# A window attention and two MLPs on one core: the first batch's attention in another order, two steps with plain float32 products, and no GpSimd work on the first block or on weights

## The chip, the core and the metric

The kernel runs on one core of one Trainium2 chip. A core has TensorE (PE in the profile, with its weight loads as PEld), VectorE (DVE), ScalarE (ACT), GpSimd (POOL) and SyncE (SP), each with an instruction queue of its own that is worked off in order, and DMA queues. All DMAs of this kernel are issued from SP. The metric is the device time of one execution in microseconds. The kernel before takes 1016.48 us (median of 3 runs, 1015.5 to 1017.78).

## The reference

Four batches of 8 heads with 512 local and 32 global tokens, head size 64. A global token attends to all 544 keys; a local token attends to the 32 global keys and to the local keys at most 32 places away. The heads are put side by side to 2176 rows of 512 (the layers after it are written for 2304 tokens; the kernel's own count is 4 x (512 + 32) = 2176).

```python
attn_out = _attn_ref(**attn_kwargs)               # softmax(q k^T / 8) v, windowed + global
x = attn_out.transpose(0, 2, 1, 3).reshape(B * S, H * D)
# _moe_ref: 512 -> 1536 -> 512
rms = np.sqrt(np.mean(x * x, axis=-1, keepdims=True) + 1e-06)
xn = x / rms * rms_g
g = xn @ w_gate
silu = g * (1.0 / (1.0 + np.exp(-g)))
x = (silu * (xn @ w_val) @ w_out).astype(np.float32)
# _moe2_ref: 512 -> 2048 -> 512
h = x @ w_in
out = (np.maximum(0.01 * h, h) @ w_out).astype(np.float32)
```

The weights of both MLPs reach the chip as float64 and everything else as float32.

## The kernel before, in words

**Weights.** A weight tile of 128 x 512 comes in as pairs of 32-bit words. `narrow` (L93) makes float32 of it in three instructions: `nc` on ScalarE (L104), `nr` on VectorE (L110) or GpSimd (L107), and `wf` on VectorE (L112). Then `split` makes two fp32r halves of it: `high` is a ScalarE cast (L75), `low` a subtraction (L83) on GpSimd for weights. A product of two float32 matrices is `mm3` (L68 to L71): three matmuls high x high, low x high, high x low.

**Blocks.** The 2176 columns (tokens) go through the first MLP in five blocks (512 and four times 416 columns), each in twelve steps f of 128 hidden units: gate `pg` and value `pv` (four mm3 each), then the product of the step before with its output weights, `yp` (four mm3). Block 0 narrows and splits each step's three weight tiles (k = 0, 1, 2 for gate, value, output) and writes the halves to `w1_dram`; blocks 1 to 4 only fetch them. The second MLP then runs over five blocks of at most 512 columns in 16 steps each (`ph`, `tl`, `h2h`/`h2l`, `o`); its own weights (`w64b`, `nr_b`, `wfb`, `w0h`, `w0l`, ...) are narrowed and split during block 4 (the first six steps' worth) and in the first 10 steps that follow.

**Attention.** Batch 0's attention runs ahead of block 0; batch b+1's is spread over block b's steps by the table `PLAN`. A unit is two heads; a half unit k has scores `S` (matmuls, VectorE min/mask L232, ScalarE exp L235), `N` (the softmax's division, L241 to L244), `T` (transposes and the copies `pt0`, `pt1` to SBUF, L257: `pt0` on ScalarE, `pt1` on VectorE) and `V` (`po`, copied into `x_loc`). `G` are the five parts of two units' global queries. The string `ORDER` lists these parts for batch 0. After each unit's `V`, `D` calls `squares` of that 128-row chunk; when the four are there `root` (L451) has TensorE sum them over partitions (`pm`), ScalarE takes the root (L459, after a table load) and VectorE the reciprocal `rv` (L461). Step 0's gate and value use `xg`, x times the gain, as two halves (L419 on GpSimd and L420 on VectorE), and its results are multiplied by `rv`; from step 1 on the operand is x normalised (`xn` L467, `xh` on ScalarE, `xl` on GpSimd).

**Order.** The kernel's text gives each engine's instructions; a scheduler that simulates the engines then decides the final order on each queue, within the dependences, the buffer counts (`bufs`) and the pins (`issue_after`, `pinned`).

Of the kernel before, what the change touches and what calls it, by code (L numbers as in the profile page):

```python
# [16 lines left out]
P = 128  # L17
# [6 lines left out]
def tile_window_global_attention_two_mlps(  # L24
# [48 lines left out]
    def high(eng, hi, src):  # L73
        if eng == "act":
            return nc.scalar.copy(hi, src)  # L75
        elif eng == "pool":
            nc.gpsimd.tensor_scalar(out=hi, in0=src, scalar1=1.0, scalar2=0.0, op0=ALU.mult, op1=ALU.add)
        else:
            nc.vector.tensor_copy(hi, src)

    def low(eng, lo, src, hi):
        e = nc.gpsimd if eng == "pool" else nc.vector
        e.tensor_tensor(out=lo, in0=src, in1=hi.bitcast(F32), op=ALU.subtract)  # L83

    def split(hi, lo, src, e_hi, e_lo):
        high(e_hi, hi, src)
        low(e_lo, lo, src, hi)
# [5 lines left out]
    def narrow(pool, dst, raw, name, e_r="dve"):  # L93

        c = pool.tile([P, DM], F32, tag="nar_c", bufs=2, name="nc_" + name)
        r = pool.tile([P, DM], U32, tag="nar_r", bufs=2, name="nr_" + name)
        nc.scalar.activation(out=c, in_=raw[:, :, 1].bitcast(F32), func=AF.Prelu, scale=2.0 ** -112,  # L104
                             alpha=-2.0 ** 32)
        if e_r == "pool":
            nc.gpsimd.tensor_scalar(out=r, in0=raw[:, :, 0], scalar1=0.93 * 2.0 ** -29, scalar2=0.03,  # L107
                                    op0=ALU.mult, op1=ALU.add)
        else:
            nc.vector.tensor_scalar(out=r, in0=raw[:, :, 0], scalar1=2.0 ** -29, scalar2=7.0,  # L110
                                    op0=ALU.mult, op1=ALU.min)
        nc.vector.scalar_tensor_tensor(out=dst.bitcast(U32), in0=c.bitcast(U32), scalar=3, in1=r,  # L112
                                       op0=ALU.logical_shift_left, op1=ALU.bitwise_or)
# [96 lines left out]
    def half_unit(k):  # L210
# [36 lines left out]
        def turned(j):  # L247
# [9 lines left out]
            (nc.vector.tensor_copy if j else nc.scalar.copy)(pt, pp)  # L257

        def values():
# [9 lines left out]
            (nc.scalar.copy if b < 2 else nc.vector.tensor_copy)(x_loc[b][:, p, c0:c0 + 2 * P], po[:, 0:2 * P])  # L269
# [83 lines left out]
    def attention(b, unit_done=None):  # L353
# [3 lines left out]
        globs = {w: global_pair(k0 // 4 + w) for w in range(NP // 2)}  # L357

        def one(t):
# [5 lines left out]
            if t[0] == "G":  # L365
                return globs[n]["1n234".index(t[2])]
# [10 lines left out]
        if not b:  # L377
            return [item(t) for t in ORDER.split()]
        return {(f, int(q)): [item(t) for t in texts.split()]
                for f, slots in PLAN.items() for q, texts in (x.split(":") for x in slots.split(";"))}  # L380

# [32 lines left out]
    def gained(c, n):  # L414
        src, g = x_loc[0][:, c, 0:n], gcol[:, c:c + 1]
        if c == 0:
            xg.extend(mp.tile([P, KC, NX], F32R, tag=f"x{y}", bufs=2, name=f"xg{y}") for y in "hl")
        hi, lo = (x[:, c, 0:n] for x in xg)
        (nc.vector if c == KC - 1 else nc.gpsimd).tensor_scalar(out=hi, in0=src, scalar1=g, scalar2=None, op0=ALU.mult)  # L419
        later(lambda: nc.vector.scalar_tensor_tensor(out=lo, in0=src, scalar=g, in1=hi.bitcast(F32),  # L420
                                                     op0=ALU.mult, op1=ALU.subtract))

    def normalise(i, c0, n):
# [40 lines left out]
        def scaled(c):  # L464
# [5 lines left out]
            high("act", xs[i][0][:, c, 0:n], xn[:, 0:n])  # L470
            later(lambda: low("pool" if i < 1 else "dve", xs[i][1][:, c, 0:n], xn[:, 0:n], xs[i][0][:, c, 0:n]))
# [14 lines left out]

    def fetch(g, k):
# [13 lines left out]

    def convert(g, k):
# [3 lines left out]
        wf[g, k] = mp.tile([P, DM], F32, tag="wf", bufs=5, name=f"wf{k}_{g}")  # L506
        with pinned({0: f"n{2 * NP - 1}", 1: "sqrt"}.get(f, "")):
            narrow(mp, wf[g, k], wraw[g, k], f"{k}_{f}", "pool" if k and f > 1 else "dve")
        if step_of(g + 1)[0] == 0:
            if g == 0:  # L510
                with tc.issue_after(loads[5, 1].ins):
                    fetch(g + 1, k)
            else:
                fetch(g + 1, k)

    def prep(g, k):

        i, f = step_of(g)
        if i == 0:
            t = weight_tile(g, k)  # L520
            split(t[:, 0, :], t[:, 1, :], wf[g, k], "act", "pool")
            nc.sync.dma_start(out=w1_dram[f][k], in_=t.bitcast(F32))
            convert(g + 1, k)

# [47 lines left out]
    def rows_in(i, c):  # L572
# [16 lines left out]

    def ahead():  # L590
# [4 lines left out]
        for f in range(6):  # L595
            for k in range(2):
                jobs.append(lambda f=f, k=k: weights2(f, k, pre2[0], mp, f"w64{(2 * f + k) % 3}"))
        for c in range(KC):
            jobs.insert(2 * (c + 1) - 1, lambda c=c: rows_in(0, c))
        return jobs  # L600

    def mlp1(early):
# [8 lines left out]
        for g in range(NI * NF1):  # L611
# [107 lines left out]
    c0 = 0  # L719
# [97 lines left out]
```

## Time and profile before

| | |
|---|---|
| time, median of 3 runs | 1016.48 us (1015.5 to 1017.78) |
| profiled execution: its own time, its span | 1016.41 us, 1014.6 us |
| mean granted TensorE clock | 0.977 |
| PE, DVE, ACT, POOL busy | 961.3, 500.5, 391.2, 159.0 us |
| first exp, last exp of batch 0's attention begin (ACT) | 6.36, 52.36 us |
| reciprocal `rv` begins (DVE) | 69.88 us |
| step 2's gate begins (PE) | 104.58 us |
| block 1 begins, second MLP begins (PE) | 219.5, 618.3 us |

The span runs from the first to the last instruction; the execution's own time has 1.8 us more, outside of all instructions. Times in the rows are us from the span's start. The granted clock is given as a share of full speed.

### The profile page before, as it was taken

What the parts mean: (1) busy time and instruction counts of PE and PEld (TensorE: products, weight loads), DVE (VectorE), ACT (ScalarE), POOL (GpSimd) and SP (SyncE); (2) the same over time, 40 slices, a digit from 0 to 9 for tenths busy, and PEclk for the clock granted to TensorE, in tenths of its full rate; (3) what the DMA queues carried; (4) which work ended last, traced back from release to release, by engine and by line L of the source; (5) the groups of instructions that cost most, each with busy time, mean ns of one, the idle gap of its engine ahead of it and who ended that gap; (6) DMA issues with size and microseconds to landing.
All of it is one profiled execution on the core that took longest, in us unless ns stands there. A gap on an engine that the chain in (4) does not pass through costs nothing.

```text
span 1014.6 us, 14017 instructions
## 1 busy us (share of the span) xinstructions
PE 961.3 (95%) x5276; PEld 830.5 (82%) x5276; DVE 500.5 (49%) x996; ACT 391.2 (39%) x895; POOL 159.0 (16%) x139
## 2 busy tenths in 40 slices
PE   6676989999999999999999999989999999999997
PEld 4554867788889988899999999668888888889996
DVE  5589877356553755453239623872322322232232
ACT  4456766444333443332125412652321322232232
POOL 2248866320000000000004200550000000000000
PEclk8797999999999999999999999989999999999999
DMA  7276999865657744557768962640200010010000
GB/s 228 92 262 229 353 327 334 309 222 186 217 181 256 224 154 158 170 192 266 235 223 309 406 205 77 209 164 0 78 1 1 27 42 1 0 52 1 1 33 22
DMA packets 55445, 163.47 MB, mean 161 GB/s; under 512 B 8656, under 2 KB 11728, under 8 KB 55376
## 3 DMA queue, kind: packets, MB, share of 16 engines
q1 hardware_dynamic: 55376, 162.56, 47.0%
q8 instruction: 42, 0.69, 0.3%
q14 instruction: 27, 0.22, 0.1%
HBM read 134.74 MB, written 27.79 MB: 160 GB/s over the span
## 4 chain that ended last, share of the span: by engine, by line
PE 48%; issue 34%; DVE 9%; DMA 5%; ACT 2%; POOL 2%; SPq 0%; DVEq 0%; ACTq 0%; POOLq 0%
PE o L71 16%; PE ph L71 16%; PE pg L71 4%; PE pv L71 4%; PE yp L71 4%; DMA w64b<-w 2%; PE po L148 1%; DVE wfb L112 1%; DVE wf L112 1%; DMA w<-w 1%; DVE nr_b L110 1%; PE sc L148 1%; ACT s_ring L235 1%; PE pp L254 1%; DMA y_dram<-ys 1%
## 5 line engine op out<-in xcount | busy, mean ns | idle before, releaser
L71 PE MATMUL pg<-xh,w 128*128 128x416 f32 (+1 forms) x472 | 136.3, 370 | 8.5 <-ACT xh L75 7.7
L71 PE MATMUL pv<-xh,w 128*128 128x416 f32 (+1 forms) x472 | 135.4, 365 | 0.0
L71 PE MATMUL yp<-hsh,w 128*128 128x416 f32 (+1 forms) x480 | 130.9, 368 | 2.9 <-ACT hsh L75 2.9
L742 DVE TENSOR_TENSOR tl<-ph,tl 128x512 f32<-128x512 f32 (+2 forms) x80 | 48.7, 610 | 159.1 <-ACT tl L741 158.7
L71 PE MATMUL ph<-ysph,w0l 128*128 128x512 f32 (+2 forms) x320 | 115.6, 361 | 0.0
L71 PE MATMUL ph<-yspl,w0h 128*128 128x512 f32 (+2 forms) x320 | 115.5, 361 | 0.0
L71 PE MATMUL ph<-ysph,w0h 128*128 128x512 f32 (+2 forms) x320 | 115.4, 361 | 0.0
L71 PE MATMUL o<-w1h,h2l 128*128 128x512 f32 x272 | 108.3, 398 | 3.9 <-DVE h2l L83 3.9
L71 PE MATMUL o<-w1l,h2h 128*128 128x512 f32 x272 | 107.6, 396 | 0.0
L741 ACT ACTIVATE tl<-ph 128x512 f32<-128x512 f32 (+2 forms) x80 | 42.6, 534 | 162.3 <-PE ph L71 161.8
L71 PEld LDWEIGHTS pg<-xh,w 128*128 128x128 f32 x472 | 86.5, 190 | 20.8 <-ACT xh L75 8.8
L71 PEld LDWEIGHTS yp<-hsh,w 128*128 128x128 f32 x480 | 90.1, 190 | 11.2 <-ACT hsh L75 3.9
L71 PEld LDWEIGHTS pv<-xh,w 128*128 128x128 f32 x472 | 88.4, 190 | 5.4 <-issue 0.9
L71 PE MATMUL o<-w1h,h2h 128*128 128x512 f32 x272 | 83.7, 394 | 2.2 <-ACT h2h L75 2.2
L71 PE MATMUL pg<-xl,w 128*128 128x416 f32 (+1 forms) x236 | 85.2, 361 | 0.0
L71 PE MATMUL pv<-xl,w 128*128 128x416 f32 (+1 forms) x236 | 85.1, 361 | 0.0
L83 POOL TENSOR_TENSOR w0l<-wfb,w0h 128x512 fp32r<-128x512 f32 x16 | 23.1, 1447 | 388.6 <-ACT w0h L75 388.6
L71 PE MATMUL yp<-hsl,w 128*128 128x416 f32 (+1 forms) x240 | 79.3, 363 | 0.8 <-DVE hsl L83 0.7
L235 ACT ACTIVATE s_ring<-s_ring,mx 128x224 f32<-128x224 f32 x128 | 60.2, 472 | 51.2 <-DVE mx L232 51.0
L83 DVE TENSOR_TENSOR h2l<-tl,h2h 128x512 fp32r<-128x512 f32 (+2 forms) x80 | 50.0, 625 | 50.6 <-ACT h2h L75 49.1
L71 PEld LDWEIGHTS ph<-ysph,w0h 128*128 128x128 f32 x320 | 60.5, 189 | 9.7
L664 DVE SCALAR_TENSOR_TENSOR th<-th,pg 128x416 f32<-128x416 f32 (+1 forms) x59 | 35.5, 602 | 66.4 <-ACT th L663 66.1
(133 smaller groups left out, 1575.6 us busy)
## 6 DMA issues: line engine op xcount, KB each, us to landing
w<-w_dram SPq DMA_DIRECT2D x144, 512.0 KB, 4.2
w<-w SPq DMA_DIRECT2D x36, 512.0 KB, 5.9
w_dram<-w SPq DMA_DIRECT2D x36, 512.0 KB, 4.5
w64b<-w SPq DMA_DIRECT2D x32, 512.0 KB, 4.4
kq<-kqv SPq DMA_DIRECT2D x32, 352.0 KB, 4.8
va<-kqv SPq DMA_DIRECT2D x16, 256.0 KB, 4.6
out<-ob SPq DMA_DIRECT2D x16, 256.0 KB, 2.1
y_dram<-ys SPq DMA_DIRECT2D x16, 208.0 KB, 3.0
```

Of the source, the lines that this page charges most:

```text
L71: nc.tensor.matmul(dst, lhs[a], rhs[b], start=first and i == 0, stop=last and i == 2)
L83: e.tensor_tensor(out=lo, in0=src, in1=hi.bitcast(F32), op=ALU.subtract)
L110: nc.vector.tensor_scalar(out=r, in0=raw[:, :, 0], scalar1=2.0 ** -29, scalar2=7.0, op0=ALU.mult, op1=ALU.min)
L112: nc.vector.scalar_tensor_tensor(out=dst.bitcast(U32), in0=c.bitcast(U32), scalar=3, in1=r, op0=ALU.logical_shift_left, op1=ALU.bitwise_or)
L148: x = nc.tensor.matmul(dst, lhs, rhs, start=start, stop=stop)
L235: nc.scalar.activation(out=sp, in_=sp, func=AF.Exp, bias=mx[:, c:c + 1], scale=-1.0, accum_out=sm[:, c:c + 1])
L254: nc.tensor.transpose(pp[:, n * P:(n + 1) * P], s[:, c0:c0 + P], ident)
L664: nc.vector.scalar_tensor_tensor(out=t, in0=t, scalar=1.0, in1=gate, op0=ALU.add, op1=ALU.mult)
L741: nc.scalar.activation(out=tl[:, 0:n], in_=pp[:, 0:n], func=AF.Copy, scale=0.01)
L742: nc.vector.tensor_tensor(out=tl[:, 0:n], in0=pp[:, 0:n], in1=tl[:, 0:n], op=ALU.max)
```

## The change

- **Batch 0's attention.** A new string `ORDER`: a half unit's transposes stand before the scores that are two ahead, the loads of units 1 to 3 and the weights of steps 0 and 1 are issued up front, and the second pair of units has its global queries moved into steps 0 and 1 of block 0 (`LAST_PAIR`, letters `P`). The copies `pt1` go to ScalarE for odd half units of batch 0 and all of batch 1.
- **Steps 0 and 1.** Their gate and value are plain float32 matmuls of `wf` and `xg` (one float32 tile, made by ScalarE), and both steps' results are multiplied by `rv`. Their halves, which later blocks need, are made in steps 1 and 2 (`kept`). When each tile is narrowed is pinned (`PINS`, `prepare`).
- **No GpSimd.** `nr` and all `low` go to VectorE, the squares to ScalarE, their sums to VectorE, as does the product of step 0 with `rv`. GpSimd is left with constants.
- **Buffers.** Two raw buffers for k = 0 and 1, seven for `wf`, one for `th`; the second MLP's early weights use the first one's buffers, and block 4's `yf` those of `sq`.

```diff
+    def low(lo, src, hi):
+        nc.vector.tensor_tensor(out=lo, in0=src, in1=hi.bitcast(F32), op=ALU.subtract)
...
-        if e_r == "pool":
-            nc.gpsimd.tensor_scalar(out=r, in0=raw[:, :, 0], scalar1=0.93 * 2.0 ** -29, scalar2=0.03,
-                                    op0=ALU.mult, op1=ALU.add)
+        nc.vector.tensor_scalar(out=r, in0=raw[:, :, 0], scalar1=2.0 ** -29, scalar2=7.0,
+                                op0=ALU.mult, op1=ALU.min)
...
-            (nc.vector.tensor_copy if j else nc.scalar.copy)(pt, pp)
+            on_act = j == 0 or b == 1 or b == 0 and k % 2
+            (nc.scalar.copy if on_act else nc.vector.tensor_copy)(pt, pp)
...
-    ORDER = ("S0 S1+N0+Q0 S2 T0+N1 V0+L22+L23+L20 T1+N2 S3 V1+D0+L21 G01+G0n S4 T2+N3 V2+L32+L33+L30 T3+N4 S5 "
-             "V3+D1+L31 G02 S6 T4+N5 G03 V4+L42+L43+L40 T5+N6 G04 S7 V5+D2+L41 G11+G1n T6+N7 V6+L52+L53+L50 T7 "
-             "V7+D3 G12+L51 G13 G14")
+    ORDER = ("S0 S1+N0+Q0 T0+N1 S2 V0 T1+N2 S3 V1+D0 G01+G0n+L30+L31 T2+N3 S4 V2 T3+N4 S5 V3+D1 G02 "
+             "T4+N5 S6 G03 V4 T5+N6 S7 V5+D2+L40+L41 G04 T6+N7 V6+L42+L43 T7 V7+D3+L52+L53")
+    LAST_PAIR = {(0, 0): "P11+P1n+L10+L11", (0, 2): "P12", (0, 3): "P13", (1, 0): "P14"}
...
+                nc.scalar.activation(out=sq[:, d:d + w], in_=src[:, c, s:s + w], func=AF.Square)
...
+                nc.scalar.activation(out=xg[0][:, c, 0:n], in_=x_loc[0][:, c, 0:n], func=AF.Copy,
+                                     scale=gcol[:, c:c + 1])
...
+    RAW = 2
...
+    PINS = {(0, 0): "n5+x4", (0, 1): "n6+x5", (1, 0): f"n{2 * NP - 1}+x6", (0, 2): f"n{2 * NP - 1}+x7",
+            (1, 1): f"n{2 * NP - 1}+x7", (2, 0): "sqrt", (1, 2): "sqrt", (2, 1): "sqrt"}
...
+    kept = [(g, k) for g in range(RAW) for k in range(2)]
...
+                if kept and 6 * g + q in (11, 13, 15, 17):
+                    halves_of(*kept.pop(0))
...
+                    if raw:
+                        nc.tensor.matmul(pp[k][:, 0:n], wf[g, k][:, c * P:(c + 1) * P], xg[0][:, c, 0:n],
+                                         start=c == 0, stop=c == KC - 1)
+                    else:
+                        mm3(pp[k][:, 0:n], [w[:, c * P:(c + 1) * P] for w in wsp[g, k]],
+                            [y[:, c, 0:n] for y in xs[i]], c == 0, c == KC - 1)
...
                     if raw:
-                        nc.gpsimd.tensor_tensor(out=t, in0=t, in1=norms[0][3]["rv"][:, 0:n], op=ALU.mult)
-                    high("act", hh, t)
-                    later(lambda t=t, hh=hh, hl=hl: low("pool" if i < 1 else "dve", hl, t, hh))
+                        nc.vector.tensor_tensor(out=t, in0=t, in1=norms[0][3]["rv"][:, 0:n], op=ALU.mult)
+                    high(hh, t)
+                    later(lambda t=t, hh=hh, hl=hl: low(hl, t, hh))
...
-    for part in range(4):
-        load(1, part)
-    for k in range(3):
-        fetch(0, k)
+    for u in (1, 2):
+        for part in range(4):
+            load(u, part)
+    for part in (2, 3):
+        load(3, part)
+    for g in range(2):
+        for k in range(3):
+            if g < W64[k]:
+                fetch(g, k)
```

What the scheduler made of it shows in the order of each queue. The first place is the start of ScalarE's queue, the first half units of batch 0's attention. `s_ring` are the score buffers (four exps to a half unit), `nc` a weight's narrowing, `pt_0`, `pt_1` the turned probabilities of half units 0 and 1, `xl` the attention's output. Before:

```order
L235 ACT_TABLE_LOAD
L235 ACTIVATE s_ring_113,sm_195<-s_ring_113,mx_194 128x224 x4
L235 ACTIVATE s_ring_114,sm_211<-s_ring_114,mx_210 128x224 x2
L104 ACTIVATE nc_0_685<-w_0_182 128x512
L235 ACTIVATE s_ring_114,sm_211<-s_ring_114,mx_210 128x224 x2
L104 ACTIVATE nc_0_693<-w_0_184 128x512
L235 ACTIVATE s_ring_115,sm_232<-s_ring_115,mx_231 128x224 x4
L257 COPY pt_0_246<-pp_0_241 128x512
L257 COPY pt_1_280<-pp_1_269 128x512
```

And now:

```order
L225 ACT_TABLE_LOAD
L225 ACTIVATE s_ring_113,sm_211<-s_ring_113,mx_210 128x224 x4
L225 ACTIVATE s_ring_114,sm_227<-s_ring_114,mx_226 128x224 x3
L248 COPY pt_0_246<-pp_0_241 128x512
L225 ACTIVATE s_ring_114,sm_227<-s_ring_114,mx_226 128x224
L225 ACTIVATE s_ring_115,sm_265<-s_ring_115,mx_264 128x224 x4
L260 COPY xl_283<-po_274 128x256
L248 COPY pt_1_290<-pp_1_285 128x512
L248 COPY pt_1_297<-pp_1_292 128x512
```

The copy `pt_0` has moved ahead of half unit 1's last exp and of all of half unit 2's, the two `nc` have left this stretch, and both copies of half unit 1 are ScalarE's.

The second place is TensorE's queue around the root: `px_g` ends the second pair's global queries, `pm` is the sum of squares, `pg` and `pv` step 0's gate and value, `sb_g` and `sa_g` the second pair's global scores, `sc_8` the first scores of batch 1. Before:

```order
L339 MATMUL px_g_672<-ident,xg_g_670 128x128
L454 MATMUL pm_676<-ssum_328,ones 128x512
L456 MATMUL pm_676<-sq_3_650,ones 128x512
L71 MATMUL pg_748<-xgh,w_0_708 128x512 x2
L71 MATMUL pg_748<-xgl,w_0_708 128x512
L71 MATMUL pg_748<-xgh,w_0_708 128x512 x2
L71 MATMUL pg_748<-xgl,w_0_708 128x512
```

And now:

```order
L443 MATMUL pm_651<-ssum_338,ones 128x512
L445 MATMUL pm_651<-sq_3_636,ones 128x512
L665 MATMUL pg_671<-xg,wf_0_524 128x512 x2
L138 MATMUL sb_g_675<-kq_2_182,bd_111 64x32
L138 MATMUL sb_g_675<-kq_3_355,bd_111 64x32
L138 MATMUL sa_g_674<-kq_2_182,bd_111 64x256
L138 MATMUL sa_g_674<-kq_3_355,bd_111 64x256
L138 MATMUL sa_g_674<-kq_2_184,bd_111 64x256
L138 MATMUL sa_g_674<-kq_3_357,bd_111 64x256
L665 MATMUL pg_671<-xg,wf_0_524 128x512 x2
L665 MATMUL pv_704<-xg,wf_0_600 128x512 x4
L138 MATMUL sc_8_757<-kq_4_566 128x224
```

The second pair's global queries have moved from ahead of the root to behind the first products of step 0, and a chunk of a gate is one matmul instruction in place of three.

The third place is VectorE's queue from just ahead of the reciprocal `rv` on; `nr` and `wf` are narrowings, `w<-wf,w` the low half of a weight, `gm_g` the global queries' maxima. Before:

```order
L431 TENSOR_TENSOR sq_3_650<-xl_267 128x512
L419 TENSOR_SCALAR xgh<-xl_267,gcol 128x512
L420 SCALAR_TENSOR_TENSOR xgl<-xl_267,gcol,xgh 128x512
L461 RECIPROCAL rv_679<-rv_679 128x512
L112 SCALAR_TENSOR_TENSOR wf_1_712<-nc_1_713,nr_1_714 128x512
L112 SCALAR_TENSOR_TENSOR wf_1_724<-nc_1_725,nr_1_726 128x512
L662 TENSOR_TENSOR gate<-pg_748,rv_679 128x512
L467 SCALAR_TENSOR_TENSOR xn_0_768<-xl_267,gcol,rv_679 128x512
```

And now:

```order
L77 TENSOR_TENSOR w_0_744<-wf_0_707,w_0_744 128x512
L450 RECIPROCAL rv_654<-rv_654 128x512
L102 SCALAR_TENSOR_TENSOR wf_2_748<-nc_2_749,nr_2_750 128x512
L102 SCALAR_TENSOR_TENSOR wf_2_796<-nc_2_797,nr_2_798 128x512
L286 TENSOR_REDUCE gm_g_683<-sb_g_675 128x1
L100 TENSOR_SCALAR nr_1_806<-w_1_713 128x512
L100 TENSOR_SCALAR nr_3_842<-w_3_649 128x512
L102 SCALAR_TENSOR_TENSOR wf_1_804<-nc_1_805,nr_1_806 128x512
L77 TENSOR_TENSOR w_2_836<-wf_2_748,w_2_836 128x512
L285 TENSOR_REDUCE gm_g_683<-sa_g_674 128x1
L77 TENSOR_TENSOR w_0_940<-wf_0_524,w_0_940 128x512
```

The squares and the halves of `xg` have left VectorE; the lows of weights and narrowings of steps 1 to 3 have come in between the reciprocal and step 0's gate.

## Rows read from the trace of the kernel before

**Rows 1.** The page: busy time of each engine.
```profile
PE 961.3 (95%) x5276; PEld 830.5 (82%) x5276; DVE 500.5 (49%) x996; ACT 391.2 (39%) x895; POOL 159.0 (16%) x139
```

**Rows 2.** Windows: span, busy PE, PEld, DVE, ACT, POOL, clock, DMA share, GB/s.
```profile
0.00:52.90 52.90, 35.13 (x262) 27.29 (x263) 28.86 (x101) 25.36 (x87) 12.17 (x31) 0.84 0.49 153
...
69.90:104.60 34.70, 23.84 (x100) 17.70 (x98) 33.90 (x47) 22.35 (x48) 26.30 (x19) 0.75 0.68 228
104.60:219.50 114.90, 111.22 (x649) 87.13 (x648) 77.36 (x147) 68.01 (x158) 64.00 (x51) 1.00 0.88 318
219.50:618.30 398.80, 394.91 (x2400) 369.07 (x2399) 203.52 (x459) 144.85 (x360) 19.20 (x13) 1.00 0.65 220
618.30:690.00 71.70, 65.69 (x269) 51.57 (x268) 48.97 (x64) 37.25 (x64) 27.91 (x20) 0.95 0.48 159
```

**Rows 3.** Waits of TensorE, 0 to 104.6 us: total us, times, longest.
```profile
PE po L148 <- DVE pt L257: 12.4, 4, 4.2
PE po L148 <- ACT pt L257: 7.8, 2, 4.7
```

**Rows 4.** Timeline of ScalarE: start, length, instruction, idle time before it.
```profile
6.36 0.48 ACT L235 ACTIVATE s_ring<-s_ring,mx 128x224 f32<-128x224 f32 x1 [4.36 <-DVE mx L232]
...
52.36 0.47 ACT L235 ACTIVATE s_ring<-s_ring,mx 128x224 f32<-128x224 f32 x1
...
67.86 1.28 ACT L459 ACT_TABLE_LOAD   x1 [1.35 <-PE pm L456]
69.16 0.69 ACT L459 ACTIVATE rv<-pm,eps 128x512 f32<-128x512 f32 x1
```

**Rows 5.** ScalarE by form, 0 to 220 us: busy us, mean ns, idle before.
```profile
L235 ACT ACTIVATE s_ring<-s_ring,mx 128x224 f32<-128x224 f32 x64 | 30.1, 472 | 24.9 <-DVE mx L232 24.8
...
L257 ACT COPY pt<-pp 128x512 f32<-128x512 f32 x16 | 9.3, 579 | 6.5 <-PE pp L254 6.5
```

**Rows 6.** Timeline of VectorE: the reciprocal.
```profile
69.88 3.35 DVE L461 RECIPROCAL rv<-rv 128x512 f32<-128x512 f32 x1 [3.10 <-ACT rv L459]
```

**Rows 7.** Timeline of TensorE: the sum of squares, step 0's value, step 2's gate.
```profile
65.89 1.03 PE L454 MATMUL pm<-ssum,ones 128*128 128x512 f32 x2
66.76 1.02 PE L456 MATMUL pm<-sq,ones 128*128 128x512 f32 x2
...
70.39 0.62 PE L71 MATMUL pv<-xgh,w 128*128 128x512 f32 x2
...
73.20 1.78 PE L148 MATMUL sc<-kq 64*128 64x224 f32 x16
...
104.58 0.74 PE L71 MATMUL pg<-xh,w 128*128 128x512 f32 x2
```

**Rows 8.** VectorE by form, 0 to 220 us: busy us, mean ns, idle before.
```profile
L112 DVE SCALAR_TENSOR_TENSOR wf<-nc,nr 128x512 uint32<-128x512 uint32 x36 | 33.8, 955 | 7.5 <-POOL nr L107 5.8 <-POOL w L83 1.2 <-ACT nc L104 0.4
L244 DVE TENSOR_TENSOR s_ring<-s_ring,sm 128x896 f32<-128x896 f32 x16 | 22.1, 1389 | 0.4
...
L110 DVE TENSOR_SCALAR nr<-w 128x512 uint32<-128x512 uint32 x16 | 16.7, 1058 | 0.5 <-DMA w<-w 0.3
...
L666 DVE SCALAR_TENSOR_TENSOR th<-th,pv 128x512 f32<-128x512 f32 x12 | 8.2, 679 | 6.6 <-PE pv L71 6.6
```

**Rows 9.** VectorE by form, 220 to 530 us, where GpSimd is idle.
```profile
L244 DVE TENSOR_TENSOR s_ring<-s_ring,sm 128x896 f32<-128x896 f32 x16 | 17.5, 1092 | 0.5
```

**Rows 10.** Timeline of VectorE, second MLP: three instructions while GpSimd is idle.
```profile
632.36 0.43 DVE L110 TENSOR_SCALAR nr_b<-w64b 128x512 uint32<-128x512 uint32 x1 [4.07 <-DMA w64b<-w]
632.70 0.69 DVE L83 TENSOR_TENSOR h2l<-tl,h2h 128x512 fp32r<-128x512 f32 x1
633.30 0.69 DVE L112 SCALAR_TENSOR_TENSOR wfb<-nc_b,nr_b 128x512 uint32<-128x512 uint32 x1
```

**Rows 11.** Waits of TensorE, 618 to 690 us: total us, times, longest.
```profile
PE o L71 <- DVE h2l L83: 3.9, 4, 1.3
PE o L71 <- ACT h2h L75: 2.2, 2, 1.8
```

More of the change, by code (lines that the diff above doesn't have):

```diff
@@ L71, in mm3, with high, split, narrow @@
             nc.tensor.matmul(dst, lhs[a], rhs[b], start=first and i == 0, stop=last and i == 2)
[L73 to L87, printed above, removed]
+    def high(hi, src):
+        nc.scalar.copy(hi, src)
+    def low(lo, src, hi):
+        nc.vector.tensor_tensor(out=lo, in0=src, in1=hi.bitcast(F32), op=ALU.subtract)
+    def split(hi, lo, src):
+        high(hi, src)
+        low(lo, src, hi)
     def words(w):
         return w.bitcast(U32).rearrange("p k (c t) -> p k c t", t=2)
-    def narrow(pool, dst, raw, name, e_r="dve"):
+    def narrow(pool, dst, raw, name):
         c = pool.tile([P, DM], F32, tag="nar_c", bufs=2, name="nc_" + name)
@@ L412, in tile_window_global_attention_two_mlps @@
     xg = []
[L414 to L421, printed above, removed]
     def normalise(i, c0, n):
@@ L505, in convert, with halves_of, prepare @@
             return
[L506 to L514, printed above, removed]
-    def prep(g, k):
[L518 to L522, printed above, removed]
-            convert(g + 1, k)
+        wf[g, k] = mp.tile([P, DM], F32, tag="wf", bufs=7, name=f"wf{k}_{g}")
+        with pinned(PINS.get((f, k), "")):
+            narrow(mp, wf[g, k], wraw[g, k], f"{k}_{f}")
+        if step_of(g + W64[k])[0] == 0:
+            fetch(g + W64[k], k)
+    def halves_of(g, k):
+        t = weight_tile(g, k)
+        split(t[:, 0, :], t[:, 1, :], wf[g, k])
+        nc.sync.dma_start(out=w1_dram[step_of(g)[1]][k], in_=t.bitcast(F32))
+    kept = [(g, k) for g in range(RAW) for k in range(2)]
+    def prep(g, k):
+        if step_of(g)[0] == 0:
+            halves_of(g, k)
+            convert(g + 1, k)
+    def prepare(g, place):
+        if g == 0:
+            if place == 1:
+                convert(0, 2)
+            elif place == 2:
+                halves_of(0, 2)
+                convert(2, 0)
+        elif g == 1 and place == 0:
+            convert(2, 1)
+            convert(1, 2)
+        elif g == 2 and place != 1:
+            if place == 2:
+                prep(3, 1)
+            prep(1 + place // 2, 2)
+        elif place:
+            prep(g + 1, place - 1)
+        else:
+            prep(g, 2)
     cols = [sum(BLOCKS1[:i]) for i in range(NI)]
@@ L660, in mlp1 @@
                     if raw:
[L661 removed]
+                        gate = mp.tile([P, NX], F32, tag="sq", bufs=2, name=f"gate{g}")[:, 0:n]
                         nc.vector.tensor_tensor(out=gate, in0=pp[0][:, 0:n], in1=norms[0][3]["rv"][:, 0:n], op=ALU.mult)
@@ L701, in tile_window_global_attention_two_mlps @@
             flush()
+        if n == 20:
+            convert(0, 0)
+        if n == 25:
+            convert(0, 1)
     flush()
     early = attention(1)
+    convert(1, 0)
     norms[0][1]()
-    for k in range(3):
-        convert(0, k)
-    for k in range(3):
-        prep(0, k)
+    convert(1, 1)
     ph_ps.close()
```

80 lines of the change are left out of this document (38 added, 42 removed).

## Prediction

> **What bounds the kernel now.** First the page's busy times: TensorE works 961.3 of 1014.6 us, the others at most half [rows 1]. So only stages in which TensorE waits or runs below full clock have something to give. The windows by stage say which [rows 2]: from 104.6 to 618.3 us TensorE is busy 111.22 of 114.90 and 394.91 of 398.80 us at clock 1.00, so the steps 2 to 11 of block 0 and all the blocks behind it hold 7.6 us of idle time together. Up to 104.6 us it is otherwise. Until 52.9 us TensorE is busy 35.13 us at 0.84 of the clock and nobody is full: VectorE 28.86, ScalarE 25.36. From 69.9 to 104.6 us VectorE is busy 33.90 of 34.70 us: it is the bound there, and TensorE's 23.84 us at clock 0.75 stand beside it. The waits name the first stage's cause: 12.4 + 7.8 = 20.2 us for the copies `pt`, with single waits of 4.2 and 4.7 us [rows 3]. Between the last exp, which ends at 52.83 [rows 4], and the reciprocal at 69.88 [rows 6] lie 17.05 us of a chain that ends in `pm` at 65.89 [rows 7], the table load and the root [rows 4]. At the head of the second MLP there are 71.70 - 65.69 = 6.0 us of idle time, and a clock of 0.95 is worth (1 - 0.95) x 71.7 = 3.6 us [rows 2]; the waits there are for `h2l` and `h2h` [rows 11].
>
> **The change part by part.** The sum goes against the profiled execution's 1016.41 us, which is 0.07 below the median of the runs.
>
> *Batch 0's attention, up to the last exp.* From the first exp at 6.36 to the end of the last at 52.83 are 46.5 us [rows 4]. In the new order ScalarE's work from its first exp to the last is 32 exps at 0.47 and 10 copies `pt` at 0.58 [rows 5], 6 copies into `xl` of half a `pt`'s columns at about 0.36, 3 squares, 2 gains and 2 narrowings of a `pt`'s size at 0.6 to 0.66, and about 2.4 of global queries: 15.0 + 5.8 + 2.2 + 4.3 + 2.4 = 29.7 us. That is one end: the last exp ends at 36.1, say 36.4, if ScalarE never waits. The other end is 52.8, no gain at all (a loss is bounded below). What speaks for a gain is the place of the copy `pt_0`: it stood behind all exps of half unit 2 and two narrowings, now it stands ahead of one exp, and the `po` matmuls that waited 20.2 us [rows 3] waited for just these copies. I take the middle, 44.6, a gain of 8.2 us: about half of those waits turn into others, since each half unit still runs through scores, exp, division, turn and value on four engines.
>
> *From the last exp to the reciprocal.* Before: 17.05 us, with the second pair's global queries, three narrowings, and the halves of `xg` between. Now: division 1.5, transposes 1.1, two copies on ScalarE 1.2, value products 1.1, copy into `xl` 0.45, two narrowings on ScalarE that stand ahead of the last square 1.3, square 0.6, hand-overs about 1, so `pm` starts 8.25 us after the last exp. Its first product takes 66.76 - 65.89 = 0.87 us for two instructions [rows 7]; ScalarE's last gain and a cast (1.2) run beside it, then the table load 1.28 and the root 0.69 [rows 4]: 11.4 to 11.7 us in all. The reciprocal starts at 44.6 + 11.7 = 56.3 in place of 69.88: 13.6 us earlier, of which 8.2 are the order's and 5.4 the chain's. Ends: 36.4 + 11.7 = 48.1 (gain 21.8) and 52.8 + 11.7 = 64.5 (gain 5.4). Below that a load that comes late in SP's queue could cost: the weights of steps 0 and 1 now stand ahead of unit 3's keys there; five of them of 0.52 MB each are 17 us of transfers at the 153 GB/s of this window [rows 2], but they need not land before half unit 6.
>
> *From the reciprocal to step 2.* VectorE is the bound, so its list counts. Up to the last `xl` it now has the reciprocal 3.35 [rows 6], 9 `wf`, 11 lows of weights, 4 `xn`, 4 `xl`, one `hsl` and 8 instructions of gate and value at a pitch of 0.61, 7 `nr` at 0.34 (the pitches from 632.36 to 632.70 and from 632.70 to 633.30 [rows 10]), 10 score instructions at an estimated 0.31, 2 divisions at 1.09 [rows 9] and some 2.3 of small ones: 3.35 + 22.6 + 2.4 + 3.1 + 2.2 + 2.3 = 36.0 us, if each runs at the length that it has with GpSimd idle. Before it was 33.90 busy of 34.70 [rows 2], with narrowings and divisions stretched: `wf` 955 against 690 ns, `nr` 1058 against 430, the division 1389 against 1092 [rows 8 to 10]. So the lows that move over take up what the shorter instructions give back. Waits I put at 2.0 (0.8 before, and as much again for the in-order queue); step 2's products can start 2.1 us (3 mm3) ahead of the last `xl`. 36.0 + 2.0 - 2.1 = 35.9, against 34.7: 1.2 lost, rounded to 1.0. TensorE's plain products cost it more: a chunk takes 2 x 0.43 = 0.86 in place of three at (73.20 - 70.39) / 12 = 0.234, 0.70 [rows 7], 16 x 0.16 = 2.5 us in two steps; VectorE's list covers it, and uncovered it would cost these 2.5 us. All of TensorE's work there is about 27 us at full clock (13.8 of plain products, 5.6 of `yp`, the rest attention), so the clock has a price too, the first rival's.
>
> That the stretched instructions are GpSimd's doing rests on this: the forms with two SBUF operands or of `nr` are longer where GpSimd works and the one that reads PSUM is not (679 ns [rows 8]; the division is shorter where GpSimd is idle [rows 9]). The Trainium skill, SBUF — State Buffer, section Who interferes with whom, has the rule behind it: VectorE and GpSimd share a pair of ports as an exclusive lock, and an instruction with two SBUF inputs or in a two-port mode blocks, or is blocked by, a GpSimd instruction for its whole length. By this rule the lengths in the new list are the short ones and the sum stands as below; by the rows alone, in which ScalarE and TensorE are busier beside the long forms too, they could stay long, which the first rival prices.
>
> *Steps 2 to 11.* VectorE takes over 24 lows of weights, 10 of `hs` and the `nr`: its list there is 81.9 us long by the same pitches, ScalarE's 82.3, against 111.22 us of TensorE in 114.90 [rows 2]. Hidden: 0. If the cover goes, it costs by the second rival. TensorE's 3.7 us of idle time there and 3.9 in the blocks after I leave as they are.
>
> *Head of the second MLP.* The waits are 3.9 for `h2l` on VectorE and 2.2 for `h2h` [rows 11]; `nr_b` and `wfb` on VectorE are no longer stretched by GpSimd's 27.91 us [rows 2], but two lows a step come to VectorE. Some narrowings of these weights moreover run earlier, at block 0's end. Ends: all 6.0 of idle time and 3.6 of clock gone (9.6), or 3 us lost if the two lows (1.2 a step) delay `h2l` in some of the ten steps. I take half of the waits, 3.0, as it is nearest to the 3.9 of VectorE.
>
> Sum: 1016.41 - 13.6 + 1.0 + 0 - 3.0 = 1000.8, about **1001 us**.
>
> **The rivals.**
> - *The front's gain is lost before step 2.* Either VectorE's instructions stay as long as beside GpSimd, though it is silent: 33 two-operand ones x 0.265 + 7 `nr` x 0.63 + 2 divisions x 0.30 = 13.7 us, to 1014.5; against it stands the division's row at 1092 ns [rows 9]. Or TensorE runs that stage at the lower of its two clocks, as before at 0.75 on average [rows 2], and its 27 us of work become up to 54: step 2 would start near where it does now, and only the 3 us at the head of the second MLP stay, about 1013. For it speaks that the clock fell in every stage where TensorE waited long; against it that plain products now keep TensorE busier than before. Together 0.14, some of it within 0.2%.
> - *Slower: VectorE's queue becomes the bound of steps 2 to 11.* It works in order, and each step has a low of `hs`, without which the next `yp` can't start, behind two or three lows and narrowings of later steps. The place is the wait of `yp` and `pg` for VectorE's lows, the price is per step: a step was 11.5 us on average [rows 2]. 13.6 - 1.0 + 3.0 = 15.6 us spread over ten steps means that from 1.6 us a step on nothing is gained; at 2.3 a step, four two-operand instructions late, it is +23 and the time 1024. For it: 81.9 of 115 us is 71% of VectorE in one order. Against it: it leaves 30 us. Chance 0.10.
> - *Bigger gain: the waits go altogether.* The last exp comes at about 41 (gain 4 more), the head of the second MLP gives 9.6 and block 0's gaps 1: 1001 - 4 - 6.6 - 1 = 989.4. Chance 0.12.
> - *The change doesn't do what it says.* The loads issued up front hold SP's queue and the first units come as late as before; then the chain's 5.4 us go into waits elsewhere: 1016. Chance 0.06.
>
> **How the numbers follow.** The forecast, 1001, has 0.58, with 995 to 1008 as its own range (the gain up to the reciprocal 13.6 +- 6, the head of the second MLP 0 to 9). For eight times in ten it reaches down to the bigger gain, 989, and up towards the lost one, 1013. About 0.2% (2 us) is what a measurement can tell from no change. Faster by more: 0.58 + 0.12 + 0.11 of the lost gain (1013 to 1014.4) = 0.81; within: 0.03 + 0.05 = 0.08; slower: 0.10 and 0.01 of the last = 0.11.
>
> **What would show it.** Right: the last exp at 40 to 48 us, the reciprocal at 52 to 60, `pm` directly behind the last square; 33 to 38 us from the reciprocal to step 2's gate with VectorE over 90% busy; `nr` near 430 and `wf` near 690 ns there; steps 2 to 11 in 112 to 116 us, and under 5 us of waits at the head of the second MLP. Wrong: an `nr` or `wf` that is still long with GpSimd silent, a clock under 0.7 between root and step 2 with TensorE full, waits of `yp` or `pg` for VectorE's lows of over 10 us in steps 2 to 11, or long waits of scores for `kq` transfers in the first 40 us.

## The result, and the profile after

The changed kernel takes 990.92 us (median of 4 runs, 989.21 to 991.91) against 1016.66 us (4 runs) of the kernel before: ratio 0.9745, 95% interval 0.9728 to 0.9763, so 25.7 us less. Forecast were 1001 (989 to 1013) and a chance of 0.81 for faster. The profiled execution's span is 987.3 us against 1014.6, 27.3 us less; the parts below are of these two executions. A second profile of the changed kernel has its reciprocal at the same 52.88 us.

The page's busy times after, against [rows 1]:

```profile
PE 950.4 (96%) x5260; PEld 817.0 (83%) x5260; DVE 494.6 (50%) x1087; ACT 400.0 (41%) x915; POOL 4.5 (0%) x26
```

VectorE has 91 instructions more and is busy 5.9 us less. The windows, cut at the same events as [rows 2] (last exp, reciprocal, step 2's gate, block 1, second MLP; columns as there):

```profile
0.00:41.10 41.10, 28.44 (x269) 22.22 (x270) 26.65 (x102) 29.62 (x97) 4.51 (x26) 0.96 0.77 248
41.10:52.90 11.80, 9.04 (x42) 5.06 (x41) 6.13 (x14) 7.91 (x16) 0.00 (x0) 0.71 0.41 137
52.90:85.80 32.90, 25.11 (x122) 14.52 (x118) 32.48 (x70) 23.60 (x56) 0.00 (x0) 0.90 0.99 355
85.80:200.20 114.40, 110.81 (x649) 86.80 (x648) 90.99 (x205) 76.47 (x175) 0.00 (x0) 1.00 0.92 333
200.20:599.70 399.50, 395.71 (x2400) 369.09 (x2399) 194.91 (x454) 138.43 (x348) 0.00 (x0) 1.00 0.62 206
599.70:671.00 71.30, 69.73 (x301) 56.02 (x300) 50.79 (x90) 40.65 (x70) 0.00 (x0) 1.00 0.56 182
671.00:987.30 316.30, 311.51 (x1489) 263.31 (x1488) 92.66 (x156) 83.32 (x157) 0.00 (x0) 1.00 0.06 21
```

Where the 27.3 us went:

| stretch | before | after | forecast | measured |
|---|---|---|---|---|
| start to the last exp's end | 52.83 | 41.15 | -8.2 | -11.7 |
| last exp to the reciprocal | 17.05 | 11.7 | -5.4 | -5.3 |
| reciprocal to step 2's gate | 34.7 | 32.9 | +1.0 | -1.8 |
| steps 2 to 11 | 114.9 | 114.4 | 0 | -0.5 |
| blocks 1 to 4 | 398.8 | 399.5 | 0 | +0.7 |
| second MLP to the end | 396.3 | 387.6 | -3.0 | -8.7 |

TensorE's waits up to 100 us, after; against [rows 3] the waits for `pt` are 5.9 + 2.0 in place of 20.2 us, and the longest of them is 1.3:

```profile
PE po L138 <- ACT pt L248: 5.9, 6, 1.3
PE pp L244 <- DVE s_ring L234: 4.4, 2, 2.8
PE pg_g L307 <- ACT sg_g L289: 4.3, 1, 4.3
PE sc L138 <- DMA kq<-kqv: 4.0, 1, 4.0
PE pz_g L138 <- ACT gt_g L312: 2.2, 1, 2.2
PE po L138 <- DVE pt L248: 2.0, 2, 1.2
```

Only part of the 20.2 us lies in the first stretch. TensorE's waits for `pt` in the kernel before, 0 to 52.9 us:

```profile
PE po L148 <- DVE pt L257: 8.2, 2, 4.2
PE po L148 <- ACT pt L257: 4.7, 1, 4.7
```

That is 12.9 us; in the changed kernel 5.9 us are left up to 41.1, and 2.8 us for the division (`s_ring`) are new. TensorE's idle time in this stretch fell by 5.1 us (17.8 to 12.7), and its busy time by 6.7 us (35.13 to 28.44 for 262 and 269 instructions) at a granted clock of 0.96 in place of 0.84. The score matmuls alone, 64 in both kernels, show it; before and after, columns: stretch, span, busy PE, PEld, DVE, clock, DMA share, GB/s:

```profile
0.00:52.90 52.90, 12.08 (x64) 8.37 (x64) 10.61 (x32) 0.84 0.49 153
0.00:41.10 41.10, 10.07 (x64) 6.88 (x64) 10.60 (x32) 0.96 0.77 248
```

So over half of this stretch's gain is TensorE's own work at a higher granted clock, with shorter waits between.

The chain after it, from ScalarE's timeline; against [rows 4] and [rows 6] the root's table load comes at 50.87 and the reciprocal at 52.88:

```profile
40.68 0.47 ACT L225 ACTIVATE s_ring<-s_ring,mx 128x224 f32<-128x224 f32 x1
...
50.87 1.28 ACT L448 ACT_TABLE_LOAD   x1
52.16 0.69 ACT L448 ACTIVATE rv<-pm,eps 128x512 f32<-128x512 f32 x1
```

VectorE by form, 0 to 200 us; the forms of [rows 8] with GpSimd silent: `wf` 687 against 955 ns, the division 1091 against 1389, `nr` 424 against 1058, and the one that reads PSUM 687 against 679:

```profile
L102 DVE SCALAR_TENSOR_TENSOR wf<-nc,nr 128x512 uint32<-128x512 uint32 x36 | 24.1, 687 | 4.8 <-ACT nc L98 4.6
...
L234 DVE TENSOR_TENSOR s_ring<-s_ring,sm 128x896 f32<-128x896 f32 x16 | 17.5, 1091 | 0.4
L100 DVE TENSOR_SCALAR nr<-w 128x512 uint32<-128x512 uint32 x36 | 14.6, 424 | 0.5 <-DMA w<-w 0.4
L687 DVE SCALAR_TENSOR_TENSOR th<-th,pv 128x512 f32<-128x512 f32 x12 | 8.2, 687 | 6.6 <-PE pv L71 6.6
```

### The profile page after: what moved, and what is told of

It is laid out like the page before. It is cut to its first block, busy times and chain, and to the rows that moved or that the text cites. A ratio compares the mean times of both kernels' runs of the same rounds, so it can differ in the third digit from the quotient of the medians.

```text
span 987.3 us, 13930 instructions
## 1 busy us (share of the span) xinstructions
PE 950.4 (96%) x5260; PEld 817.0 (83%) x5260; DVE 494.6 (50%) x1087; ACT 400.0 (41%) x915; POOL 4.5 (0%) x26
## 5 line engine op out<-in xcount | busy, mean ns | idle before, releaser
L71 PE MATMUL pg<-xh,w 128*128 128x416 f32 (+1 forms) x464 | 131.8, 365 | 0.8 <-DVE th L685 0.8
L71 PE MATMUL pv<-xh,w 128*128 128x416 f32 (+1 forms) x464 | 131.2, 361 | 0.0
L71 PEld LDWEIGHTS pg<-xh,w 128*128 128x128 f32 x464 | 84.2, 188 | 11.7 <-issue 5.9
L71 PEld LDWEIGHTS pv<-xh,w 128*128 128x128 f32 x464 | 86.1, 188 | 4.9 <-issue 1.3
L71 PE MATMUL pv<-xl,w 128*128 128x416 f32 (+1 forms) x232 | 83.1, 358 | 0.0
L71 PE MATMUL pg<-xl,w 128*128 128x416 f32 (+1 forms) x232 | 83.0, 358 | 0.0
L71 PEld LDWEIGHTS ph<-yspl,w0h 128*128 128x128 f32 x320 | 60.1, 188 | 9.4
```

The source lines that it names most:

```text
L71: nc.tensor.matmul(dst, lhs[a], rhs[b], start=first and i == 0, stop=last and i == 2)
```

## The experiments

Times are medians; the kernel before ran beside each on the same chip (1014.7 to 1018.8), so ratios are compared. 0.1% is 1 us.

**The order alone, in the kernel before.**

```diff
-    ORDER = ("S0 S1+N0+Q0 S2 T0+N1 V0+... T1+N2 S3 V1+... G01+G0n S4 T2+N3 V2+... T3+N4 S5 ...
+    ORDER = ("S0 S1+N0+Q0 T0+N1 S2 V0+... T1+N2 S3 V1+... G01+G0n T2+N3 S4 V2+... T3+N4 S5 ...
```

> The kernel before with one part of the change: batch 0's transposes ahead of the scores two on, as in the new order; the second pair stays ahead of the root, loads, GpSimd's work and the early narrowings stay as they were. Theory (the interleaving alone is most of the 11.7 us up to the last exp, as its undoing in the changed kernel suggests): last exp at 43 to 47 us, time -5 to -9. Rival (the order helps only with the other parts: GpSimd stretches the divisions and the narrowings stand between the exps): last exp at 49 to 53, time 0 to -3.

Measured 1005.57, ratio 0.9882 (0.9854 to 0.9910): 12 us less, more than either expected. ScalarE's timeline of this kernel, the last exp:

```profile
41.34 0.47 ACT L235 ACTIVATE s_ring<-s_ring,mx 128x224 f32<-128x224 f32 x1
```

It ends at 41.8, within 0.7 of the changed kernel and earlier than expected, with the narrowings still between the exps and GpSimd's work in place. The chain from there to the reciprocal is 19.4 us (61.2), 2.3 longer than before. The order gives 11.0 of the 11.7 us in the first row of the table.

**The order undone in the changed kernel.**

```diff
-    ORDER = ("S0 S1+N0+Q0 T0+N1 S2 V0 T1+N2 S3 V1+D0 ... T2+N3 S4 V2 T3+N4 S5 V3+D1 G02 T4+N5 S6 ... T5+N6 S7 ...
+    ORDER = ("S0 S1+N0+Q0 S2 T0+N1 V0 T1+N2 S3 V1+D0 ... S4 T2+N3 V2 T3+N4 S5 V3+D1 G02 S6 T4+N5 ... T5+N6 S7 ...
```

> The changed kernel with batch 0's attention in the old interleaving (scores two ahead before the transposes), with everything else of the change, loads included. Theory (the place of the copies pt behind the exps is what TensorE waited for): the last exp comes 5 to 9 us later (46 to 50 us) and the time is +5 to +9. Rival (GpSimd's and the narrowings' absence shortened this stretch): last exp within 2 us of 41, time +0 to +2.

Measured 998.06, ratio 0.9816 (0.9789 to 0.9844), some 7 us over the changed kernel. The profiled execution was its longest (1001.61). There the last exp ends at 51.0, a microsecond later than expected, the reciprocal is at 62.3, and TensorE's longest waits up to 62 us are again those for `pt`:

```profile
PE po L138 <- DVE pt L248: 11.4, 4, 5.7
```

These are the copies on VectorE. In VectorE's queue three of the four stand behind an `sm` that itself waited 1.1 us for the next half unit's exps; so they too came behind exps, though no exp is in their own queue.

**The second pair's global queries ahead of the root again.**

```diff
-             ... V5+D2+L40+L41 G04 T6+N7 V6+L42+L43 T7 V7+D3+L52+L53")
-    LAST_PAIR = {(0, 0): "P11+P1n+L10+L11", (0, 2): "P12", (0, 3): "P13", (1, 0): "P14"}
+             ... V5+D2+L40+L41 G04 G11+G1n T6+N7 V6+L42+L43 T7 V7+D3+L52+L53 G12+L50+L51 G13 G14")
+    LAST_PAIR = {}
```

> The changed kernel with the second pair's global queries ahead of the root, as before the change. Theory (the chain from the last exp to the root and VectorE's list behind it are both on the path): root 4 to 6 us later, stage from the reciprocal to step 2 shorter by about 2 us of VectorE's work, time +2 to +4. Rival (only the total of VectorE's work counts): root later by as much as the stage behind is shorter, time within 1 us.

Measured 994.74, ratio 0.9787 (0.9760 to 0.9814), about 4 over. The reciprocal comes 2.8 us later (55.7), less than expected. Step 2's gate begins at 85.5, so the stage between the two is 3.1 us shorter; but the last `xl` ends at 91.9 in place of 87.9, and step 2's value comes 5.3 us and step 3's 4.1 us later. TensorE's 6.5 us of waits for the second pair (`sg_g`, `gt_g`) gave way to one of 5.8 us for `hsh`. The rival, time within 1 us, is out.

**Low halves of block 0's weights back on GpSimd.**

```diff
-        split(t[:, 0, :], t[:, 1, :], wf[g, k])
+        split(t[:, 0, :], t[:, 1, :], wf[g, k], "pool")
```

> The changed kernel with the low halves of block 0's weights on GpSimd again (36 subtractions; nr, xl, hsl, squares stay where the change put them). Theory (shared access): VectorE's list from the reciprocal to step 2 loses 11 x 0.61 = 6.7 us and gets most of it back by longer wf, nr and divisions, so the stage stays at 31 to 35 us and the time within 3 us of the changed kernel (989 to 994). Rival (VectorE's list counts and GpSimd's work is free): the stage falls by 5 to 7 us to 26 to 28, the time to 984 to 986.

Measured 997.83, ratio 0.9808 (0.9780 to 0.9836): 6 us over, outside of both. The window from the reciprocal to step 2's gate of this kernel:

```profile
52.70:91.10 38.40, 26.27 (x129) 14.86 (x127) 35.28 (x62) 24.94 (x58) 17.09 (x11) 0.82 0.92 346
```

and VectorE by form from 52 to 120 us:

```profile
L103 DVE SCALAR_TENSOR_TENSOR wf<-nc,nr 128x512 uint32<-128x512 uint32 x18 | 16.5, 931 | 0.3
L101 DVE TENSOR_SCALAR nr<-w 128x512 uint32<-128x512 uint32 x16 | 11.3, 729 | 0.0
```

VectorE has 8 instructions fewer (62 for 70) and is busy longer (35.28 for 32.48): eleven subtractions that GpSimd takes over (17.09 us there) cost VectorE more than they take off it. TensorE loses most of the time at one wait, 8.3 us where the changed kernel has 2.2; ScalarE's copy `gt_g` stands behind a narrowing that waits 2.9 us for VectorE's `wf`:

```profile
PE pz_g L139 <- ACT gt_g L313: 8.3, 1, 8.3
```

**Low halves of the second MLP's weights back on GpSimd.** The same edit in `weights2`.

> The changed kernel with one part undone: the low halves of the second MLP's weights are GpSimd's again, all else (buffers, early narrowing) stays. Theory (GpSimd blocks VectorE's two-operand and nr forms, and TensorE waits for h2l behind them): most of the 8.8 us that the second MLP gained come back, +5 to +9 against the changed kernel (996 to 1000 us), nr_b and wfb beside GpSimd at 1.2 to 1.6 us, waits of o for h2l and h2h of 4 to 6 us, clock dip. Rival (the gain is that of the earlier narrowings and buffers): 0 to +1.5, head idle as in the changed kernel.

Measured 1001.53, ratio 0.9847 (0.9822 to 0.9873): 10 over. VectorE by form, 604 to 680 us of this kernel:

```profile
L103 DVE SCALAR_TENSOR_TENSOR wfb<-nc_b,nr_b 128x512 uint32<-128x512 uint32 x20 | 21.8, 1089 | 4.5 <-ACT nc_b L99 3.3
L101 DVE TENSOR_SCALAR nr_b<-w64b 128x512 uint32<-128x512 uint32 x20 | 12.5, 623 | 5.0 <-DMA w64b<-w 4.9
L78 DVE TENSOR_TENSOR h2l<-tl,h2h 128x512 fp32r<-128x512 f32 x12 | 10.8, 900 | 2.5 <-ACT h2h L74 2.3
```

The changed kernel has 685, 426 and 688 ns there. TensorE waits for `h2l` and `h2h` again, 7.0 us, against 1.6 in the changed kernel:

```profile
PE o L71 <- DVE h2l L78: 3.9, 6, 1.3
PE o L71 <- ACT h2h L74: 3.1, 3, 1.7
```

The second MLP takes 395.0 us here, so 7.4 of the 8.7 come back with these lows. Of the blocks ahead of it, 1 to 4 are 5 us longer, 3.3 of them at one wait of a gate for VectorE in block 4 (4.1 us in place of 0.8), where the first of these lows are made. The clock did not dip (1.00), against what was expected.

**The same part alone, in the kernel before.** `"pool"` to `"dve"` in `weights2`.

> The kernel before with one part of the change: the low halves of the second MLP's weights on VectorE in place of GpSimd, nothing else. Theory (GpSimd's work there blocked VectorE): the second MLP gets all or most of its 8.8 us, time -6 to -9 (1008 to 1011). Rival (the earlier narrowings and buffers of the change are needed, and two more lows a step load VectorE): -3 to +2.

Measured 1011.49, ratio 0.9953 (0.9931 to 0.9974): 5 us less, between the two expectations. The second MLP takes 391.3 against 396.3; no wait for `h2l` is left, 3.7 us for `h2h` are. So the lows alone give 5.0 of the 8.7. The other 3.7 need the rest of the change; that it is the earlier narrowings and not the buffers is not shown.

**GpSimd's effect by itself.** 72 additions and 72 memsets that nothing needs, in the changed kernel.

```diff
+                        for _ in range(6):
+                            if i == 1:
...
+                                nc.gpsimd.tensor_tensor(out=scr, in0=mk[:, 0:336], in1=mk[:, 336:672], op=ALU.add)
+                            elif i == 2:
+                                nc.gpsimd.memset(scr, 1.0)
```

> The changed kernel with work for GpSimd that nothing needs: behind each step's gate six additions of two 336-column tiles from SBUF in block 1, six memsets of 336 columns (which read nothing) in block 2, nothing in block 3. The disputed cost by itself. Theory (exclusive use by instructions that read SBUF): in block 1 hsl (584 ns) and the division of the softmax (1091 ns) get longer by 0.2 to 0.6 us where they overlap, th with a PSUM operand does not; in block 2 nothing gets longer. Rival (any GpSimd instruction slows VectorE, by power or by the write side): block 2 shows it too. Time of the kernel within 2 us of the changed one, TensorE being the bound there.

They did not land where they were meant to: nothing held them back on GpSimd's queue, and they ran from 5.4 to 89.7 us (additions) and from 89.7 to 122.4 (memsets). So the blocks that were meant show nothing, but block 0 does, with the same work on the other engines beside it. The one execution took 1011.59 us, 20 over in place of within 2, with step 0's value 21 us late. VectorE by form beside the additions:

```profile
L236 DVE TENSOR_TENSOR s_ring<-s_ring,sm 128x896 f32<-128x896 f32 x8 | 12.6, 1578 | 0.2
L100 DVE TENSOR_SCALAR nr<-w 128x512 uint32<-128x512 uint32 x12 | 12.4, 1050 | 0.0
L102 DVE SCALAR_TENSOR_TENSOR wf<-nc,nr 128x512 uint32<-128x512 uint32 x10 | 12.2, 1237 | 1.3 <-ACT nc L98 1.3
...
L250 DVE COPY pt<-pp 128x512 f32<-128x512 f32 x4 | 2.7, 686 | 0.9 <-PE pp L246 0.9
```

and beside the memsets:

```profile
L102 DVE SCALAR_TENSOR_TENSOR wf<-nc,nr 128x512 uint32<-128x512 uint32 x7 | 4.7, 679 | 0.6 <-ACT nc L98 0.6
L100 DVE TENSOR_SCALAR nr<-w 128x512 uint32<-128x512 uint32 x7 | 3.8, 571 | 0.0
L236 DVE TENSOR_TENSOR s_ring<-s_ring,sm 128x896 f32<-128x896 f32 x3 | 3.2, 1083 | 0.0
```

Beside additions, which read SBUF, the two-operand forms and `nr` are longer by 0.5 to 0.6 us on average and the copy from PSUM is not; beside memsets, which read nothing, the two-operand forms are not, and `nr` is (571 for 424). By the Trainium skill, SBUF — State Buffer, section Who interferes with whom, a VectorE instruction with two SBUF inputs contends with a GpSimd instruction that reads SBUF and not with one that only writes, while one in a two-port mode contends with GpSimd without that exception. The runs agree, if `nr` runs in such a mode; no run here shows that it does.

**Step 0 in plain float32, in the kernel before.** One `xg` by ScalarE and `wf` as weights.

> The kernel before with step 0's gate and value as plain float32 products of wf and one float32 xg that ScalarE makes (no xgh on GpSimd, no xgl on VectorE); its halves are still made where they were. Expected by the theory that the chain to the root was lengthened by GpSimd's xgh and VectorE's xgl (3 x 2.1 and 4 x 1.0 us): root 1 to 4 us earlier, TensorE +1.2 us hidden, time -1 to -4. Rival (the chain is that of the attention, and the halves were hidden): within 1 us.

Measured 1012.58, ratio 0.9962 (0.9939 to 0.9985): 4 us less by the times. The profiled execution, 1016.95, was one of its longer ones and has the reciprocal at 70.4, no earlier than before. In it the last exp ends at 49.9, 2.9 us earlier, but the 20.4 us from there on ran at a granted clock of 0.67, where the kernel before had 0.90. Where the 4 us come from is open.

**Three attempts at more.** `xn`, `xh`, `xl` asked for in step 0:

```diff
-                    if g:
-                        run(scaled, (1, 1, 1, 1, 0, 0)[q])
+                    if not g:
+                        run(scaled, (0, 2, 2, 0, 0, 0)[q])
```

> A version meant to be better than the changed kernel: step 1's and later steps' normalised x (xn, xh, xl) is asked for in step 0 in place of step 1, so that VectorE does it ahead of weights of later steps. If VectorE's order (and not its whole list) sets step 2's start: step 2 2 to 4 us earlier and the time -1 to -4. If the whole list is what counts, weights included: within 1 us.

Measured 991.99, ratio 0.9757 (0.9731 to 0.9782): the same. Then the same edit with pins, without and with the halves of steps 0 and 1 made later (in the diff the first line is of the pins, the rest of the later halves; the first expectation is that of the pins alone, and its "version before" is the one with both, whose expectation follows):

```diff
+            (2, 2): "xn0_3", (3, 0): "xn0_3", (3, 1): "xn0_3"}
...
+    KEPT_AT = (25, 31, 37, 43)
...
-                if kept and 6 * g + q in (11, 13, 15, 17):
+                if kept and 6 * g + q in KEPT_AT:
```

> As the version before, but the halves of steps 0 and 1 stay where the change put them (steps 1 and 2): list up to the last xl 22.9 us. If VectorE's order is all, as good as the other (-3 to -6); if the four casts, lows and writes of 2 MB to HBM count, 1 to 3 us behind it.

> Meant to be better than the changed kernel, and a test of VectorE's list as the bound from the reciprocal to step 2: xn, xh, xl are asked for in step 0, the narrowings of step 3 and of step 2's output weights are pinned behind the last xn, and the halves of steps 0 and 1 that only later blocks need are made from step 4 on (their float32 tiles lie in a buffer that is free until then). VectorE's list up to the last xl falls from 35.8 to 21.7 us by the same lengths. If that list is the bound, TensorE's own 25 to 27 us are next and step 2 starts 4 to 7 us earlier, the time -3 to -6 against the changed kernel. If the transfers (16 engines busy 0.99 of that stage) or the whole list up to step 4 are the bound: within 1 us.

> The changed kernel on the same chip as the two versions, for their comparison: 989 to 993 us, ratio to the kernel before 0.973 to 0.977.

On one chip: 988.44 with the pins (ratio 0.9728, 0.9705 to 0.9752), 994.24 with the later halves too (0.9779, 0.9751 to 0.9808), 990.04 the changed kernel (0.9742, 0.9713 to 0.9771). The pins' 1.6 us are within the intervals, so no version is shown to beat the changed one, and the gain of 3 to 6 us that both expectations held out did not come. Windows of the kernel with the pins alone:

```profile
52.80:84.00 31.20, 23.81 (x98) 13.36 (x94) 30.23 (x65) 21.93 (x53) 0.00 (x0) 0.84 0.90 311
84.00:105.00 21.00, 20.49 (x127) 16.57 (x128) 20.68 (x52) 16.54 (x41) 0.00 (x0) 1.00 1.01 390
105.00:132.00 27.00, 26.51 (x159) 19.99 (x158) 23.23 (x58) 19.80 (x49) 0.00 (x0) 1.00 0.99 362
```

Behind the reciprocal, VectorE's list up to the last `xl` was 12 us shorter (22.8 for 35.0 us), yet step 2's gate began at 86.5 in place of 85.2 and step 2's value came at 94.8 in place of 95.1. So that list was not what held step 2. TensorE's waits in this kernel from 52.8 to 86.5 us, all that there are:

```profile
PE pz_g L138 <- ACT gt_g L312: 4.1, 1, 4.1
PE pg_g L307 <- ACT sg_g L289: 2.5, 1, 2.5
PE po L138 <- ACT pt L248: 1.2, 1, 1.2
```

The changed kernel has the same three in its stage, 2.2, 4.3 and 1.2 us. They are all of TensorE's idle time there (32.90 - 25.11 = 7.8), and none is for `xl`: TensorE's own work and the waits inside the second pair's global queries fill the stage. VectorE acts on it through those waits, as the lows on GpSimd showed. From 84 us on TensorE is busy nearly throughout (20.49 of 21.00 and 26.51 of 27.00 us). A version without those waits was tried only in the kernel with the pair ahead of the root, where another wait took their place.

No run takes these parts of the change by themselves: the plain products of steps 0 and 1 in the changed kernel, the copies `pt1` on ScalarE, the loads up front, the buffers.

## Why the prediction was right or wrong

- *Direction and mechanisms: right in the main.* Beside GpSimd's work on SBUF VectorE's instructions are longer, and copies `pt` that come behind exps held TensorE; each was shown by undoing it, the order and the second MLP's lows also alone, in the kernel before. The measured 990.9 us lie in the stated range but below the forecast's own 995 to 1008. They are where the rival "bigger gain" stood (989.4, chance 0.12), with the last exp at about 41 us and most of the 9.6 us at the second MLP. The waits did not go altogether, as that rival had it.
- *Batch 0's attention: right mechanism, a size off, 8.2 for 11.7.* The term that was mis-sized is the middle between two ends, "about half of those waits turn into others". Its row was not that of the stretch: of the 20.2 us of waits 12.9 lie ahead of the last exp. There TensorE's idle time fell by 5.1 us only. The other 6.7 us are its own work at a granted clock of 0.96 in place of 0.84, for which this term had nothing. The middle was a choice without a row behind it.
- *The chain to the reciprocal: right*, 5.4 for 5.3. Moving the second pair is 2.8 us of it by its undoing; no run separates the rest.
- *Reciprocal to step 2: +1.0 for -1.8.* A small loss was forecast and a small gain came. VectorE's list was counted right: it took 34.6 us for 36.0, its waits 0.4 for 2.0, and the last `xl` ends at 87.9, 35.0 us behind the reciprocal. But the step "VectorE is the bound, so its list counts" failed: with that list 12 us shorter step 2 began no earlier, and TensorE's 25.1 us of work and 7.8 us of waits for `sg_g`, `gt_g` and `pt` make up the stage. That the list's sum, 35.9 us, came near the measured 32.9 is then in part luck.
- *Steps 2 to 11: right.* VectorE's 90.99 us (forecast 81.9, so 9 too few) lay under TensorE's 110.81; the slower rival did not occur.
- *Head of the second MLP: the largest miss, 3.0 for 8.7.* "Two lows a step come to VectorE" was counted as a price of up to 3 us. The undoing shows no such price: the two lows cost VectorE 1.4 us a step, and GpSimd's absence gives back 0.40 + 0.20 us for each pair of `wfb` and `nr_b`, of which a step has two, and 0.21 for `h2l`, 1.4 in all (1089, 623, 900 to 685, 426, 688 ns), on the path to `h2l`. The clock's 3.6 us were in the upper bound only; the changed kernel has 1.00 there. Over the whole second MLP TensorE's idle time fell by 5.3 us and its busy time by 3.4 (384.7 to 381.2), so both parts of that bound came for the most part. Its end in the kernel before, the row that [rows 2] lacks:

```profile
690.00:1014.60 324.60, 319.00 (x1522) 269.38 (x1520) 94.11 (x158) 84.57 (x159) 0.00 (x0) 1.00 0.06 20
```

- *The rival of long VectorE forms* is refuted by 424, 687 and 1091 ns. That of the lower clock did not occur: 0.90 in that stage.

## What to carry to other kernels

Read which copy a waiting matmul waits for and what stands ahead of it in its engine's queue: issuing each half unit's transposes and their copies ahead of the next scores and exps gave 12 us with no instruction less. Before a wait's row prices a stage, cut the row to that stage, and look at the granted clock beside it: here TensorE's own work got shorter by more than its idle time. Where VectorE is full, a two-operand instruction given to GpSimd can cost VectorE more than it saves, so compare the same form's mean length with and without GpSimd beside it before offloading. And a full engine is not yet the bound: shorten its list and see whether the next stage moves.

## What was not expected of the hardware

Eleven subtractions less on VectorE made it busy 2.8 us longer. A 4-element `sm` instruction took 600 ns beside GpSimd's additions and 168 without. And one program's first stage is not the same length each time: the kernel with the second MLP's lows on VectorE has the same VectorE list as the kernel before up to block 4, and its reciprocal came at 74.8 us in its profiled execution, 69.9 in the other. Of these 4.9 us 3.4 lie between the last exp and the reciprocal, where the granted clock was 0.67 in place of 0.90 and the same 87 matmuls kept TensorE busy 15.1 in place of 11.6 us. Why the clock differed is open, and it bounds how finely two single profiles can be compared there.
